# One-core transformer block on Trainium2: projections, transposes and state reads as two row tiles of 64, with new operation orders

## The chip, the cores and the metric

The kernel runs on one core of a Trainium2 chip. A core has TensorE (PE: matmuls and transposes into PSUM, PEld: its weight loads), VectorE (DVE), ScalarE (ACT), GpSimd (POOL), and SyncE (SP), which issues nearly all DMA transfers. The metric is the device time of one execution in microseconds, the median of several runs: 807.32 us before (three runs, 806.09 to 807.65).

## The reference

One transformer block on x of 2048 rows and 512 columns: layer norm with scale and shift from a conditioning vector, attention with a compressive memory, a residual, a second layer norm, a feed-forward part, a residual. The attention has 32 heads of 16 columns and runs in 4 segments of 512 rows:

```python
...
for s in range(N):
    qs, ks, vs = q[:, :, s], k[:, :, s], v[:, :, s]
    logits = jnp.einsum("bhqd,bhkd->bhqk", qs, ks) * scale + mask
    p = _softmax(logits, axis=-1)
    a_dot = jnp.einsum("bhqk,bhkd->bhqd", p, vs)
    pq = phi(qs)
    num = jnp.einsum("bhld,bhde->bhle", pq, M)
    den = jnp.einsum("bhld,bhd->bhl", pq, z)[..., None] + 1e-6
    a_mem = num / den
    o = g * a_mem + (1.0 - g) * a_dot
    pk = phi(ks)
    M = M + jnp.einsum("bhld,bhle->bhde", pk, vs)
    z = z + jnp.einsum("bhld->bhd", pk)
...
h = jnp.einsum("bsf,fd->bsd", relu(x @ w1 + b1) ** 2, w2) + b2
...
```

phi(t) is t + 1 above zero and exp(t) below. The masks are causal within a segment.

## The kernel before

**Tiles and stages.** A unit u (16 of them: segment s = u // 4, column block cc = u % 4) is 8 heads of one segment, that is 128 columns. Products are made from a high and a low part of each operand, so that a product over 128 rows takes three matmuls: high x high, high x low, low x high. For each unit:

- `qk(u)` projects q and k (w = 0, 1): four steps k over 128 rows each, three matmuls of 512 columns per step, into one PSUM bank for q and one for k. ScalarE and VectorE split each bank into the high and low part `sg`; SyncE writes them by 12 transfers (`fill`) into the slots of `ST`, in which two heads of 16 columns lie in each half of 64 partitions. For the memory, ScalarE and GpSimd make phi(q) and phi(k).
- `vproj(s)`, once per segment, projects v for four row blocks t in the same way; ScalarE copies the result into `VT`.
- `a_quad(u, qd)`, for each half of the heads, makes the scores once for the row maxima (`mmA`, 63 rows per matmul, two matmuls beside each other for partitions 0 to 63 and 64 to 127). VectorE reduces; TensorE transposes the maxima, ScalarE negates them (`mt`), and SyncE writes them into `ST` (`rows`).
- `b_quad(u, qd)` makes the scores again with the maxima in a further row (`score`, 64 rows per matmul, in such pairs); ScalarE takes the exponential, GpSimd applies the mask (`select`), `pv` multiplies with v in four column tiles of 32. ScalarE copies the output (`oraw`), TensorE transposes it (`turn_o`), and VectorE divides (`norm`).
- `mem(u)` reads the memory for phi(q) (`read`, 128 rows, 136 columns, four row blocks), transposes phi(k) (`tr`) and updates the memory (`upd`, column tiles of 32).

After that, `wo_tile(g)` multiplies by wo for 16 row blocks, `ln2` makes the second layer norm's operand H2 in one of two buffers, and `ffn1` and `ffn2` run the feed-forward part with w1 and w2 in the same three matmuls per step. 70 warm-up matmuls of a constant stand at the start.

**What sets the order.** The code doesn't run its operations as it writes them. It creates a list of operations (`op`: engine, planned cost, function, priority `pr`, dependencies `after`, buffers to take and give back `get`, `put`). `Plan.run` goes through a written order for each engine (`ORDER`, numbers of operations as they are created), with planned costs, latencies and, for TensorE, a planned cost of each change of mode (`TURN`; F: the whole 128 x 128 array, R: two row tiles of 64, C: four column tiles of 32). `Plan.emit` then calls the functions in that order. On TensorE, VectorE, ScalarE and GpSimd the emitted order is what runs. For SyncE the framework's own scheduler decides. PSUM has eight banks, which the plan hands out; an operation waits on the chip for the banks and buffers that it takes over.

The planned costs are the code's own numbers. The prediction doesn't draw on them.

Of the kernel before, what the change touches and what calls it, by code (L numbers as in the profile page):

```python
# [8 lines left out]
F32 = mybir.dt.float32  # L9
F32R = mybir.dt.float32r  # L10
# [47 lines left out]
8 59 76 43 58 57 16 68 17 53 14 25 35 51 3 33 62 70 10 47 30 34 75 26 20 46 49 69 48 71 19 50 28 11 38 63 74 56 23  # L58
15 67 42 41 65 21 37 39 22 52 73 86 13 105 94 64 88 29 96 60 12 24 72 77 111 40 31-32 36 18 45 117 27 54 123 161 171
162-164 172 165 173 166 174 167 175 168 324 176-178 325-326 330-331 205 213 332 221 206 214-215 327 207 333 216 208  # L60
222-223 229 243 224 480 736 486 240 237 481 197 487 198 488 234 249 482 269 246 199 483 257 352 489 200 254 273
609-610 280 263 271 603 283 260 604 363 288 611 425 266 741 605 276 360 606 612 66 44 372 366 292-294 298 357 301
305 308 55 296 9 369 61 383 313 380 508 751 746 519 427 317-318 386 429 513 319 396 522 436 755-756 439 444 377 757
321 548 758 765 389 516 528 404 550 536 432 533 766-767 406 859 768 525 448 631 639 454 449-450 412 461 642 457 398
920 542 464 469 671 921 414 452 539 645 473 420 474-475 552 636 559 922 477 923 787 861 788-789 545 790 803-804 651
662 567 930-931 555 562 665 805 648 932 992 933 806 422 994 571 656 577 580 673 572 819 659 584 573 596 587 592 833
575 1053-1054 668 1055 675 839 824 597-598 678 682 830 1056 863 1063 600 1064 690 685 827 1065-1066 795-797 836 798
853 850 952 694-696 700 703 707 1339 1125 811-812 1127 813 698 814 957 710 966 715 719 865 847 868 720-721 875 871
844 1186 996 723 1187 856 878 963 972 1188 883 960 986 1189 1196-1197 1334 1198 969 1199 977 887-888 893 980 896 889
998 900 983 1085 1093 908 903 891 1129 989 912 1329 1099 1105 1096 913 1001 1110 914 1131 1004 1090 1008 1116 1016  # L70
1011 1262 916 1102 1344 1113 1020-1022 1026 1119 1218 1033 1258 1348 1358 1029 1036 1223 1349 1260 1024 1122 1359
# [148 lines left out]


class Node:
    __slots__ = ("eng", "dur", "lat", "fn", "pr", "mode", "get", "put", "left", "outs", "seq", "nb", "at")


class Plan:
# [1115 lines left out]
```

## Time and profile before

| quantity | value |
| --- | --- |
| median of three runs | 807.32 us |
| span of the profiled execution | 804.3 us |
| TensorE matmul records, busy | 792.1 us |
| VectorE busy | 537.3 us |
| ScalarE busy | 440.5 us |
| GpSimd busy | 232.9 us |
| matmuls, and as many weight loads | 5289 |
| granted TensorE clock | 1.000 |

The span runs from the first to the last instruction of one profiled execution. The runs are timed without a profile; the profiled execution has no time of its own beside its span. Attention takes the first 460 us or so, with `wo_tile` and the weights' preparation in its last part, and the feed-forward part the rest. A matmul's record lasts longer than its share of TensorE, because matmuls are pipelined; start to start is the measure of what it costs. A float32 matmul (PV, state reads, state update) has two records.

### The profile page before, as it was taken

The page shows a single profiled execution, that of the slowest core. Times are in us where ns is not written, and L with a number is a line of the kernel's source. Part 1 is how long each engine was busy: PE and PEld are TensorE (multiplying, and loading weights), DVE is VectorE, ACT ScalarE, POOL GpSimd, SP SyncE. Part 2 cuts the span into 40 slices and gives each one's busy share as a digit, 9 for nine tenths or more (in the row PEclk, how much of TensorE's full clock was granted, in tenths as well). Part 3 has the DMA queues.
Part 4 walks back from the last instruction along what each step waited for, and adds up shares of the span by engine and source line. Part 5 has one row for each costly group of instructions (what it writes and reads, how often), then busy time and mean ns, then how long its engine had stood idle before and what let it go on. Part 6 is the DMA issues. An engine that isn't in the chain of part 4 may idle for free.

```text
span 804.3 us, 14894 instructions
## 1 busy us (share of the span) xinstructions
PE 792.1 (98%) x5289; PEld 582.3 (72%) x5289; DVE 537.3 (67%) x1425; ACT 440.5 (55%) x908; POOL 232.9 (29%) x314
## 2 busy tenths in 40 slices
PE   8999999999999999999999999999999999999998
PEld 7876666676666756665766678788888888888886
DVE  4688888779877797777999879864433434424223
ACT  1648866789867896677665744543233323322211
POOL 4555535537655684444332211000000000000000
PEclk9999999999999999999999999999999999999999
DMA  9655562324214442434622143230100010001001
GB/s 309 174 135 123 156 206 71 87 74 107 75 47 106 107 103 54 99 74 99 172 66 80 54 145 105 92 92 13 53 1 0 1 53 0 1 1 53 1 1 52
DMA packets 51300, 65.23 MB, mean 81 GB/s; under 512 B 7829, under 2 KB 24985, under 8 KB 51226
## 3 DMA queue, kind: packets, MB, share of 16 engines
q1 hardware_dynamic: 51074, 64.14, 28.6%
q8 instruction: 42, 0.69, 0.3%
q14 instruction: 32, 0.26, 0.1%
q10 hardware_dynamic: 152, 0.13, 0.1%
HBM read 29.91 MB, written 7.34 MB: 46 GB/s over the span
## 4 chain that ended last, share of the span: by engine, by line
PE 80%; DVE 10%; ACT 4%; DMA 3%; issue 2%; SPq 1%; POOL 1%; DVEq 0%; ACTq 0%; POOLq 0%
PE bpv L1015 7%; PE bpf L1291 6%; PE bpf L1290 6%; PE bpf L1292 6%; PE bh L1264 6%; PE bh L1262 6%; PE bh L1263 6%; PE bpb L956 5%; PE ba L799 5%; PE bqk L711 4%; PE bqk L712 3%; PE bqk L713 3%; DVE ba L804 2%; PE bv L770 2%; PE bwop L1101 2%
## 5 line engine op out<-in xcount | busy, mean ns | idle before, releaser
L804 DVE CUSTOM_DVE_ANT_0 ba<-ba,msk 128x512 f32<-128x512 f32 (+2 forms) x384 | 192.5, 532 | 31.0 <-PE ba L799 23.5
L973 ACT ACTIVATE pt<-bpb 128x512 f32<-128x512 f32 x320 | 171.4, 627 | 30.4 <-PE bpb L956 26.6
L1279 DVE TENSOR_TENSOR r<-r 128x512 f32<-128x512 f32 x56 | 38.7, 691 | 122.2 <-ACT rr L1276 122.1
L1272 ACT ACTIVATE r<-bh,b1c 128x512 f32<-128x512 f32 x56 | 38.5, 687 | 138.6 <-PE bh L1264 97.7
L960 POOL TENSOR_SCALAR_AFFINE_SELECT pt<-pt 128x512 f32<-128x512 f32 x128 | 80.1, 645 | 113.1 <-ACT pt L973 86.7
L1291 PE MATMUL bpf<-W,rr 128*128 128x512 f32 x224 | 88.1, 394 | 0.0
L1290 PE MATMUL bpf<-W,rr 128*128 128x512 f32 x224 | 88.1, 393 | 0.0
L1292 PE MATMUL bpf<-W,rr 128*128 128x512 f32 x224 | 87.6, 391 | 0.0
L1015 PE MATMUL bpv<-pt,VT 128*32 128x512 f32 (+3 forms) x1024 | 80.6, 437 | 0.2 <-DVE mx L804 0.2
L956 PE MATMUL bpb<-ST 64*128 64x256 f32 (+2 forms) x512 | 74.5, 353 | 1.3 <-ACT ac L832 0.4
L799 PE MATMUL ba<-ST 63*128 63x256 f32 (+2 forms) x512 | 73.2, 354 | 1.0 <-DVE mx L804 0.7
L956 PEld LDWEIGHTS bpb<-ST 64*128 64x128 f32 x512 | 46.9, 185 | 27.2 <-issue 6.6
L799 PEld LDWEIGHTS ba<-ST 63*128 63x128 f32 x512 | 44.2, 185 | 30.9 <-issue 10.5
L711 PE MATMUL bqk<-HT,WQK 128*128 128x512 f32 (+1 forms) x136 | 58.7, 431 | 0.2 <-DVE sg L732 0.2
L1276 ACT ACTIVATE rr<-r 128x512 fp32r<-128x512 f32 x56 | 35.4, 632 | 41.2 <-PE bpf L1292 40.1
L804 DVE DVE_READ_ACCUMULATOR2_ANT mx<- 128x1 f32 x384 | 54.1, 141 | 0.1
L712 PE MATMUL bqk<-HT,WQK 128*128 128x512 f32 (+1 forms) x136 | 51.9, 382 | 0.7 <-DVE HT L595 0.7
L713 PE MATMUL bqk<-HT,WQK 128*128 128x512 f32 (+1 forms) x136 | 51.8, 381 | 0.0
L1015 PEld LDWEIGHTS bpv<-pt,VT 128*32 128x32 f32 x1024 | 27.2, 109 | 33.7 <-issue 27.3
L1290 PEld LDWEIGHTS bpf<-W,rr 128*128 128x128 f32 x224 | 42.1, 188 | 9.8
L1291 PEld LDWEIGHTS bpf<-W,rr 128*128 128x128 f32 x224 | 42.0, 188 | 9.6
L1292 PEld LDWEIGHTS bpf<-W,rr 128*128 128x128 f32 x224 | 42.1, 188 | 9.4
(160 smaller groups left out, 1614.1 us busy)
## 6 DMA issues: line engine op xcount, KB each, us to landing
ST<-sg SPq DMA_DIRECT2D x192, 128.0 KB
wr<-in_B_w SPq DMA_DIRECT2D x28, 256.0 KB
xt<-in_A_x SPq DMA_DIRECT2D x16, 256.0 KB
wm<-in_w_mod SPq DMA_DIRECT2D x16, 256.0 KB
xw<-in_A_x SPq DMA_DIRECT2D x16, 256.0 KB
o_dram<-on SPq DMA_DIRECT2D x12, 256.0 KB
ot<-o_dram SPq DMA_DIRECT2D x12, 256.0 KB
out<-X SPq DMA_DIRECT2D x12, 256.0 KB
```

Of the source, the lines that this page charges most:

```text
L711: nc.tensor.matmul(p[:, c], wh, HT[:, 0, k, c], start=(k == 0), stop=False)
L712: nc.tensor.matmul(p[:, c], wh, HT[:, 1, k, c], start=False, stop=False)
L713: nc.tensor.matmul(p[:, c], wl, HT[:, 0, k, c], start=False, stop=(k == KD - 1))
L799: nc.tensor.matmul(dst[:, c0:c0 + n], ST[b:b + 63, 0, sl, qt * P:(qt + 1) * P], ST[b:b + 63, 1, sl, :n], start=True, stop=True)
L804: nc.vector.tensor_tensor_reduce(i, i, msk[:, 512 - n:], scale=1.0, scalar=-3e38, op0=ALU.add, op1=ALU.max, accum_out=o)
L956: nc.tensor.matmul(dst, ST[b:b + 64, 1, sl, kb * P:(kb + 1) * P], ST[b:b + 64, 0, sl, q0:512], start=True, stop=True)
L960: nc.gpsimd.affine_select(out=ap, in_=ap, pattern=[[0, ap.shape[1]], [1, P]], compare_op=ALU.is_ge, fill=0.0, base=0, channel_multiplier=-1)
L973: ns = [act(512, lambda j=j: nc.scalar.activation(buf("PPP"[n], pt)[:, i + j], bank(keys[j]), AF.Exp, scale=0.25), pr[slot] + 0.01 + 0.001 ...
L1015: nc.tensor.matmul(bank(o)[32 * hq:32 * hq + 32, q0:q0 + src.shape[1]], v[:, a:a + 32], src, start=start, stop=stop, tile_position=(0, 32 ...
L1290: nc.tensor.matmul(p, rh, FF["W2"][:, f, 0], start=(f == 0), stop=False)
L1291: nc.tensor.matmul(p, rh, FF["W2"][:, f, 1], start=False, stop=False)
L1292: nc.tensor.matmul(p, rl, FF["W2"][:, f, 0], start=False, stop=(f == NF - 1))
```

## The change

What it does:

1. `qk(u)` for u > 0 and `vproj(s)`: each step's three matmuls over 128 rows become six over 64 rows, in pairs for the two halves of the partitions. In the first half of the operation (turn 0), the lower half of the partitions adds into the first bank and the upper half into the second; in turn 1 they swap. The two banks are those of q and k, or of two row blocks of v, which are now made together. Between the turns a one-element copy on ScalarE (`fence`) rewrites an element that turn 1 reads.
2. The transposes of the row maxima, of phi(k) and of the attention output, and the reads of the memory: two row tiles of 64 into two banks. The output of a unit is transposed in one operation for both of its halves instead of two. A half `qd` now has the head pairs qd and qd + 2 in place of 2 qd and 2 qd + 1, and a slot of `ST` follows `slot(u, pp)`.
3. SyncE joins the engines whose order is kept as written.
4. The plan: new costs for some operations and mode changes, dependencies that hold for the plan's start order only (`soft`), a limit for transfers under way, and the rewrite of H2 planned after all of its readers (`F1[s - 2, f]` for every f) instead of the last one.
5. All written orders are new. The warm-up matmuls all stand ahead of the last steps of the first projection.

```diff
...
+    def fence(cell, pr, n):
+        return op("ACT", 0.06, lambda: nc.scalar.copy(cell, cell.bitcast(F32)), pr, after=[n])
+    def slot(u, pp):
+        return (4 * u + 2 * (pp % 2) + pp // 2) % NSLOT
...
+        def half(turn, k):
+            for i, (x, y) in enumerate(((0, 0), (0, 1), (1, 0))):
+                for j in (1, 0) if turn else (0, 1):
+                    w, r = j ^ turn, slice(64 * j, 64 * j + 64)
+                    nc.tensor.matmul(bank(banks[w]), W3(w, k, x, cols.start, cols.stop)[r], HT[r, y, k], start=turn == k == i == 0,
+                                     stop=turn == 1 and k == 0 and i == 2)
...
+            for turn in (0, 1):
+                for k in range(KD):
+                    if turn and not k:
+                        n = fence(HT[64:65, 0, KD - 1, :1], pr[0] + 0.01, n)
+                    n = pe("R", 0.697, lambda turn=turn, k=k: half(turn, KD - 1 - k if turn else k), pr[turn] + 0.002 * k,
...
-        for t in range(4):
-            b = ("v", s, t)
...
+        for t2 in (0, 2):
+            banks = [("v", s, t2 + i) for i in (0, 1)]
+            def mm(turn, k, t2=t2, banks=banks):
+                for i, (x, y) in enumerate(((0, 0), (0, 1), (1, 0))):
+                    for j in (1, 0) if turn else (0, 1):
+                        t, r = j ^ turn, slice(64 * j, 64 * j + 64)
+                        nc.tensor.matmul(bank(banks[t]), HT[r, x, k, (t2 + t) * P:(t2 + t + 1) * P], WVO[r, k, y],
+                                         start=turn == k == i == 0, stop=turn == 1 and k == 0 and i == 2)
...
-        n = pe("F", 0.03, lambda: nc.tensor.transpose(bank(b)[:16, :P], TL[mx], ident), p_tail, after=reds, get=[("#D", b)],
+                nc.tensor.transpose(bank(b[j])[:16, :64], TL[mx][r], ident[r, r])
...
-                    nc.tensor.matmul(qv[:, i], TL[q_][:, t * P:(t + 1) * P], MB[:, cc], start=True, stop=True)
+                        nc.tensor.matmul(bank(banks[j])[:, t * w:(t + 1) * w], TL[q_][r, t * P:(t + 1) * P],
+                                         MB[r, cc, j * w:(j + 1) * w], start=True, stop=True)
...
-                    nc.tensor.transpose(bank(b)[:, t * P:(t + 1) * P], TL[f][:, t * P:(t + 1) * P], ident)
+                        nc.tensor.transpose(bank(b[j])[:, t * 64:t * 64 + 64], TL[f][r, t * P:(t + 1) * P], ident[r, r])
...
-                nc.tensor.transpose(bank(b)[:, t * P:(t + 1) * P], TL[r][:, t * P:(t + 1) * P], ident)
+            for q in (0, 1):
+                for t in range(4):
+                    for j in (0, 1):
+                        w = slice(64 * j, 64 * j + 64)
+                        nc.tensor.transpose(bank(b[j])[:, t * P + 64 * q:t * P + 64 * q + 64], TL["oraw", u, q][w, t * P:(t + 1) * P],
+                                            ident[w, w])
...
-            ln2(s, [z + ST2 * ((s - 1) * NF + 4 + 2 * t) for t in range(4)], [F1[s - 2, NF - 1]] if s > 1 else WOL)
+            ln2(s, [z + ST2 * ((s - 1) * NF + 4 + 2 * t) for t in range(4)], [F1[s - 2, f] for f in range(NF)] if s > 1 else WOL)
...
-    with tc.manual_schedule(engines={mybir.EngineType.PE, mybir.EngineType.DVE, mybir.EngineType.Activation, mybir.EngineType.Pool}):
+    with tc.manual_schedule(engines={mybir.EngineType.PE, mybir.EngineType.DVE, mybir.EngineType.Activation, mybir.EngineType.Pool, mybir.EngineType.SP}):
...
```

More of the change, by code (lines that the diff above doesn't have):

```diff
@@ L63 @@
[L63 to L67, printed above, removed]
@@ L248, in op @@
         n.outs, n.left, n.seq, n.at = [], 0, len(self.nodes), None
-        for a in after:
+        n.soft = {a.seq for a in soft}
+        for a in (*after, *soft):
             if a is not None:
@@ L354, in run @@
                 for o in n.outs:
-                    same = o.eng == n.eng and not n.nb
+                    same = o.eng == n.eng and not n.nb or n.seq in o.soft
                     c = 0 if same else 1 if o.eng != "PE" else 2 if o.mode != "R" else 3
@@ L895, in mem @@
[L895 to L902 removed]
+            banks = [("mr", u, j) for j in (0, 1)]
```

520 lines of the change are left out of this document (273 added, 247 removed), and 10 rows, old and new, of the table ORDER.

## The prediction

> **What bounds the kernel now.** I read the page first: busy shares, slices, chain.
>
> ```profile
> span 804.3 us, 14894 instructions
> PE 792.1 (98%) x5289; PEld 582.3 (72%) x5289; DVE 537.3 (67%) x1425; ACT 440.5 (55%) x908; POOL 232.9 (29%) x314
> ...
> PEclk9999999999999999999999999999999999999999
> ...
> PE 80%; DVE 10%; ACT 4%; DMA 3%; issue 2%; SPq 1%; POOL 1%; DVEq 0%; ACTq 0%; POOLq 0%
> ```
>
> TensorE bounds it: 98% busy, at nine tenths of its clock or more in every slice, and 80% of the chain of waits. But consecutive matmul records overlap (0.40 us long, 0.23 apart), so "busy" also covers time in which the array streams nothing. That time shows only from start to start, which the timeline of TensorE gives (start, length, line, tiles, shape). Four stretches hold what is needed:
>
> ```profile
> 402.65 0.40 PE L1103 MATMUL bwop<-WVO,oT 128*128 128x512 f32 x1
> 402.98 0.50 PE L956 MATMUL bpb<-ST 64*128 64x256 f32 x4
> 403.32 0.63 PE L799 MATMUL ba<-ST 63*128 63x512 f32 x4
> 403.88 2.36 PE L1015 MATMUL bpv<-pt,VT 128*32 128x512 f32 x32
> 406.17 0.73 PE L956 MATMUL bpb<-ST 64*128 64x512 f32 x4
> 406.73 0.46 PE L799 MATMUL ba<-ST 63*128 63x256 f32 x4
> ```
>
> Changes between score pairs and the v projection:
>
> ```profile
> 336.25 0.40 PE L956 MATMUL bpb<-ST 64*128 64x512 f32 x2
> 336.57 0.50 PE L770 MATMUL bv<-WVO,HT 128*128 128x512 f32 x1
> 336.91 0.40 PE L771 MATMUL bv<-WVO,HT 128*128 128x512 f32 x1
> ```
>
> Score pairs in a row:
>
> ```profile
> 76.94 0.51 PE L956 MATMUL bpb<-ST 64*128 64x512 f32 x2
> 77.28 0.40 PE L799 MATMUL ba<-ST 63*128 63x512 f32 x2
> 77.51 0.49 PE L956 MATMUL bpb<-ST 64*128 64x512 f32 x2
> ```
>
> The v projection in a row:
>
> ```profile
> 245.36 0.40 PE L771 MATMUL bv<-WVO,HT 128*128 128x512 f32 x1
> 245.60 0.40 PE L772 MATMUL bv<-WVO,HT 128*128 128x512 f32 x1
> 245.83 0.39 PE L770 MATMUL bv<-WVO,HT 128*128 128x512 f32 x1
> ```
>
> Call 128x128 work F, work in row tiles of 64 (scores) R, work in column tiles of 32 (PV, state update) C. Within F a 512-wide matmul takes 0.235 (245.36, 245.60, 245.83), three of them 0.70. Within R two matmuls of 64 rows and 512 columns together also take 0.235 (77.28 to 77.51). At a change of mode it is more. F to R: 402.65 to 402.98 is 0.33, 0.095 too much, and the first R operation 0.34 where I fit 0.238, 0.10 more: 0.195 in all. R to F: 336.25 to 336.57 is 0.32 and 336.57 to 336.91 is 0.34: 0.19. R to C and back: the three PV steps take 0.86, 0.86 and 0.43, 2.15, but 403.88 to 406.17 is 2.29, 0.14 more; the two score pairs before them take 0.56 instead of 0.47, and the next pairs (406.17 to 406.73) about 0.10 more than their share: 0.33 for both changes. Over all operations I fitted 0.198 (RF), 0.197 (FR), 0.115 (RC), 0.216 (CR) and 0.20 for FC and for CF.
>
> The order list that the kernel prints gives the changes of mode: 69 RF, 63 FR, 42 RC, 48 CR, 15 FC, 9 CF; the trace alternates exactly so. That is 46 us, almost all of it before 480 us. Work within a mode makes 714 us, 487 of it in 696 triples of 0.70. So 760 of the 804 us are work and mode changes; 44 are the start, waits and the tail.
>
> **The change, part by part.** *Mode changes.* Projections, state reads, transposes of phi(k), of the attention output and of the row maxima turn from F to R, and the order is new. I numbered the operations as the code creates them and counted along the new list: 27 RF, 28 FR, 52 RC, 51 CR, 5 FC, 6 CF, 169 instead of 246. The difference: 42 RF and 35 FR fewer, 15.2 us; 10 RC and 3 CR more, 1.8 us; 10 FC and 3 CF fewer, 2.6 us. **-16.0.**
>
> *Projections.* 120 + 64 operations keep their columns: three F matmuls of 512 become three pairs of 64-row matmuls. Rows of score pairs give 0.235 a pair, so 0.70 for 0.70. With twice the instructions and loads I take +0.4; from 0 to +1.3 if all pairs land at 0.237. Untold by these rows: score pairs write with start and stop set, whereas the new pairs add to what stands in PSUM. F matmuls that add keep 0.235, which is the nearest row; the contrary is a rival below.
>
> *Transposes and state reads.*
>
> ```profile
> 244.69 0.60 PE L1043 MATMUL bfin<-ident,oraw 128*128 128x128 f32 x4
> 245.05 0.48 PE L770 MATMUL bv<-WVO,HT 128*128 128x512 f32 x1
> ...
> 264.93 0.62 PE L884 MATMUL bmr<-MB,phi 128*128 128x136 f32 x4
> 265.30 0.48 PE L711 MATMUL bqk<-HT,WQK 128*128 128x512 f32 x1
> ```
>
> An output transpose takes 0.36, two per unit, 32 in all. Afterwards a unit has 16 of half the width, two at a time: between half of 0.71 (if columns count) and all of it (if loads count). I take the middle, 0.53: 16 x 0.18 = -2.9 (-5.7 to 0). The same for phi(k): 12 x (0.36 to 0.27) = -1.0 (-2.1 to 0). State reads are 24 x 0.37; then twelve times eight matmuls of half the width. Half to one and a half of 0.75: I take no difference (-4.5 to +4.5). The transposed row maxima, 32 of 0.03, stay small.
>
> *The turn in the middle.* Every new projection pair swaps its two banks half way, with a one-element ScalarE copy between: 15 for q/k, 8 for v. TensorE's next half waits for it, in order, and so does whatever is listed behind it.
>
> ```profile
> L862 ACT ACTIVATE mt<-bat x32: 248/261/268, 57.6 to 450.5; 16x128 fp32r<-16x128 f32 x32
> ...
> L973 ACT ACTIVATE pt<-bpb 128x512 f32<-128x512 f32 x320 | 171.4, 627 | 30.4 <-PE bpb L956 26.6
> ```
>
> A small ScalarE instruction takes 0.26; the last matmul ends 0.40 after its start, 0.165 beyond its slot; with 0.15 (estimate) for the two hand-overs, 0.6 must be covered. The new list puts 0.29 to 5.5 us of other TensorE work there, under 0.6 in four of the 23, under 0.9 in eleven. ScalarE is in order too: behind half an exponential (0.31) the uncovered sum is 2.5 us, with none 0.5, behind a whole one 6.4. **+2.5.** Uncovered altogether it would be 23 x 0.6 = 14. The copies, 32 further row-maximum copies and 12 further phi(k) copies add some 17 us to ScalarE at 0.26 each; its 45% of idle time hides that.
>
> *SyncE.* Its issues, transfers of segment fills and row maxima among them, now follow the list. At the start this matters:
>
> ```profile
> 3.60 6.63 DMA X1L<-in_A_wq
> 10.25 8.21 DMA wmod<-in_w_mod
> ```
>
> ```profile
> 26.00 0.38 PE L711 MATMUL bqk<-HT,WQK 128*128 128x256 f32 x1
> ```
>
> The first two lines are of the chain of waits: the modulation waits for its weights until 18.46, and wq's transfer stands ahead of them. The third is the timeline's first q/k matmul. The new list issues all modulation weights ahead of wk, wv and wq: the modulation can come earlier by up to wq's 6.63 us, the q/k weights come later. By the list TensorE reaches the first q/k step after 18.0 us of work instead of 20.2, 22 on the clock with the 4 us by which it then lags its list now, not 26. But unit 0's first score also needs its six segment fills on SyncE. I take **-2** (-4 to +3).
>
> *Nothing on the path:* new planner costs, soft dependencies, and the wait for all readers of the feed-forward operand. TensorE runs its list in order, and the last reader comes last on it; what covers the rewrite is the next segment's first product, 56 operations of 0.70. Without that cover, its ScalarE and VectorE steps would show between segments.
>
> **Sum:** -16.0 + 0.4 - 2.9 - 1.0 + 2.5 - 2.0 = -19.0 on the span of 804.3: 785.3. The median shown, 807.32, lies 3.0 above this span: **788.3 us**. What can be told from no change here is 0.2%, 1.6 us. Adding the bounds in root-sum (3 for the output transposes, 4.5 reads, 4 turns, 4 start, and 11 for the waits of a new order, a quarter of the 44): about 13 either way, 775 to 801.
>
> **Rivals.** *B, the gain is partly given back as waits.*
>
> ```profile
> 180.00:200.00 20.00, 19.96 (x225) 12.20 (x224) 18.95 (x64) 18.81 (x43) 15.42 (x22) 1.00 0.44 108
> ...
> 380.00:400.00 20.00, 19.85 (x160) 13.61 (x161) 19.38 (x57) 13.54 (x28) 7.92 (x10) 1.00 0.65 180
> 400.00:420.00 20.00, 20.00 (x167) 13.11 (x164) 18.46 (x55) 12.95 (x26) 6.70 (x10) 1.00 0.26 80
> 420.00:440.00 20.00, 20.00 (x147) 13.05 (x146) 19.07 (x62) 12.96 (x27) 4.44 (x8) 1.00 0.24 81
> ```
>
> Columns: stretch, its length, then busy time of TensorE, its loads, VectorE, ScalarE, GpSimd. In these 80 us VectorE has 18.5 to 19.4 of 20 in use. If it can't give more, a share of 80/460 of the gain, 3.3 us, is lost there, and waits beside them double it: 795. Against it: the stretches on either side can take VectorE's work, which is 67% over the span. *C, the waits shrink as well.* The planner now charges GpSimd and VectorE steps what they take, so the new order could lose a third of the 30 us or so of waits (44 less the start and the tail): 778. No row shows it.
>
> *D, slower: pairs that add to PSUM don't fully overlap.* Place: the 184 projection operations. Full overlap 0.70, none 1.40. It decides from 19/184 = 0.10 us each, a loss of 15% of the overlapped rate; at half overlap, +0.35 x 184 = +64: 852. For it: no row has adding row tiles. Against it: score pairs overlap fully, and column tiles of PV add at full rate (0.86 for four of 512). The Trainium skill (TensorE: Matmul & The Clock Gate, Measured speedup vs the span model) reports 3.07x for four row tiles instead of 4x. By that factor an operation would take 0.91 and the kernel some 827 us; the trace's score pairs, 0.235 for two where F has 0.235 for one, disagree.
>
> *E, slower: the turns stall.* If ScalarE's queue holds the copy behind instructions that wait themselves, each turn costs more; the gain is gone at 0.83 us more for each of the 23. At 1.5 more: 823. Against it: 11 turns have over a microsecond of cover. *That the change doesn't do what it says* is no case for the modes, which can be counted; for SyncE's order it is: little moves, and the 2 us are missing, within the forecast's range.
>
> **How the numbers follow.** Forecast 0.60, B 0.14, C 0.12, D 0.05, E 0.09. Faster: forecast, C, and nearly all of B: 0.84. Slower: D, E and a little of B: 0.13. Same 0.03. For the range I leave out D, E's upper part and C's lower end: 775 to 805.
>
> **What would show it.** Right: about 169 changes of mode on TensorE, projection pairs 0.235 apart start to start, a first q/k matmul near 22 us, attention's last PV step some 19 us earlier than now, a feed-forward part as long as now. Wrong: projection pairs over 0.27 apart (D); idle TensorE ahead of the second halves with ScalarE as releaser (E); VectorE or ScalarE over 95% with TensorE waiting for them in the middle (B).

## The result, and the profile after

| | before | after |
| --- | --- | --- |
| median of 20 runs each | 807.57 us (806.09 to 811.02) | 803.85 us (800.68 to 807.82) |
| span of the profiled execution | 804.3 us | 805.9 us |

The ratio of the times is 0.9951, 95% interval 0.9939 to 0.9964: 0.5% faster, 3.7 us, where 19 us were forecast. 803.85 lies inside the range of 775 to 805, at its end. The profiled execution of the changed kernel is one of its longest (807.64) and that of the kernel before one of its shortest (the times lie 1.7 us above the spans, so 804.3 answers to 806.0), so the spans differ by +1.6 us where the medians differ by -3.7, and some 5 us of what is longer after in the parts below belong to these two executions.

The page of the changed kernel, the lines that answer to those of before:

```profile
span 805.9 us, 16640 instructions
PE 777.3 (96%) x6145; PEld 591.0 (73%) x6145; DVE 532.0 (66%) x1425; ACT 447.8 (56%) x975; POOL 230.5 (29%) x314
...
PEclk9999999999999899998999999999999999999998
...
PE 76%; DVE 6%; ACT 5%; DMA 5%; issue 3%; SPq 3%; POOL 1%; DVEq 0%; ACTq 0%; POOLq 0%
```

Three things are new: TensorE is busy for 15 us less, its granted clock falls under nine tenths in three slices, and the chain that ended last has more of DMA and of SyncE's queue (SPq) in it.

The windows view (length, then busy time of TensorE, its loads, VectorE, ScalarE, GpSimd; clock; DMA) of the changed kernel at the joints of the segments, where one segment's attention runs out and the next one's projections begin:

```profile
160.00:180.00 20.00, 17.59 (x199) 11.90 (x191) 15.35 (x46) 16.14 (x37) 12.58 (x17) 1.00 0.39 93
...
260.00:280.00 20.00, 18.11 (x168) 11.67 (x164) 11.49 (x41) 17.34 (x39) 11.21 (x14) 0.84 0.34 80
360.00:380.00 20.00, 16.74 (x162) 10.36 (x163) 17.91 (x53) 14.43 (x31) 9.59 (x12) 0.90 0.55 157
380.00:400.00 20.00, 20.00 (x166) 12.43 (x159) 17.76 (x50) 12.36 (x26) 6.61 (x8) 0.92 0.52 132
```

and of the kernel before:

```profile
160.00:180.00 20.00, 19.85 (x191) 14.17 (x184) 15.75 (x56) 16.58 (x37) 7.37 (x15) 1.00 0.30 78
...
260.00:280.00 20.00, 20.00 (x178) 14.13 (x176) 16.09 (x55) 16.45 (x36) 13.79 (x19) 1.00 0.44 108
360.00:380.00 20.00, 19.85 (x136) 12.39 (x135) 15.36 (x45) 14.71 (x34) 8.11 (x11) 1.00 0.43 104
```

In these three stretches TensorE had no matmul running for at most 0.15 of 20 us before; now it is 1.9 to 3.3. From 60 to 80 it is busy for 17.16 of 20 us where it was for 19.55.

I fitted the start-to-start times of all of TensorE's operations again, in the way of the prediction: a duration for each kind, a price for each kind of change of mode, and the rest as waits. "Tail" runs from the start of the last operation (three matmuls) to the end of the span.

| us | before | after | difference | forecast |
| --- | --- | --- | --- | --- |
| work within a mode | 713.5 | 709.0 | -4.5 | -3.5 |
| changes of mode (246, 169) | 46.1 | 33.5 | -12.6 | -16.0 |
| waits | 38.3 | 49.7 | +11.4 | +2.5 and -2.0 |
| tail | 4.8 | 12.2 | +7.4 | 0 |
| sum | | | +1.7 | -19.0 |

At the prices of the kernel before, the 169 changes are 30.1 us and the waits 53: the fit gives R to C 0.182 where it was 0.115, and can't tell a dearer change from a wait that stands beside it; 3 us or so can stand on either line. The first two lines bring 17.1 of the 19.5 us that were forecast for them; the last two take it back. With the medians' -3.7 us in place of +1.7, and the other three lines as they are, the waits grow by about 6 us instead of 11.4 (an estimate).

**The tail.** SyncE's stores at the end of the changed kernel, from the timeline (start, length, engine, line, operation, count; the second column is that of the whole group):

```profile
725.12 2.41 SPq L1363 DMA_DIRECT2D out<-X  x5
796.84 0.81 SPq L1363 DMA_DIRECT2D out<-X1L  x2
797.69 0.45 SPq L1363 DMA_DIRECT2D out<-X  x1
798.24 0.40 SPq L1363 DMA_DIRECT2D out<-X1L  x1
798.68 1.64 SPq L1363 DMA_DIRECT2D out<-X  x3
800.36 0.64 SPq L1363 DMA_DIRECT2D out<-X1L  x1
801.05 1.33 SPq L1363 DMA_DIRECT2D out<-X  x2
```

X1L is the last segment, X the others. After five stores at 725 none is issued for 69 us, and ten are left when the last tile is ready. The kernel before has four left there, all of X1L, and the first of them is issued 0.9 us ahead of the last matmul's start (799.94), here 2.7 us behind it (794.17):

```profile
799.04 2.37 SPq L1302 DMA_DIRECT2D out<-X1L  x4
```

VectorE's list has a part in it. The last additions of the changed kernel, then the matmul that ends last:

```profile
794.60 2.55 DVE L1361 TENSOR_TENSOR X1L<-bpf,X1L 128x256 f32<-128x256 f32 x5 [5.35 <-PE bpf L1353]
```

```profile
794.17 0.39 PE L1353 MATMUL bpf<-W,rr 128*128 128x512 f32 x1
```

The group begins with a half tile, 256 columns: tile 3 of the segment, the one that TensorE finishes last. VectorE waits 5.35 us for it while tiles 1, 0 and 2 lie finished.

**The clock.** Windows of 3.41 us of the changed kernel, laid on the edges of the clock's record (the column after the engines is the granted clock); each stretch at half clock has the window ahead of it:

```profile
72.41:75.83 3.42, 1.41 (x12) 0.62 (x12) 2.51 (x8) 1.65 (x5) 3.42 (x4) 1.00 0.08 26
75.83:79.24 3.41, 3.41 (x50) 1.74 (x53) 0.00 (x0) 2.23 (x5) 1.40 (x2) 0.50 0.00 0
270.38:273.80 3.42, 2.57 (x22) 1.16 (x18) 3.28 (x15) 2.54 (x6) 2.52 (x2) 1.00 0.21 43
273.80:280.63 6.83, 5.79 (x37) 2.96 (x36) 5.09 (x19) 6.43 (x14) 3.17 (x5) 0.50 0.04 13
372.78:376.20 3.42, 0.90 (x9) 0.76 (x9) 3.38 (x8) 2.54 (x6) 1.79 (x2) 1.00 0.23 75
376.20:383.03 6.83, 6.76 (x44) 4.12 (x48) 5.31 (x15) 4.67 (x12) 3.22 (x4) 0.50 0.29 79
```

TensorE is busy for 1.41, 2.57 and 0.90 of 3.42 us, then it gets half its clock for one or two such windows: 17 us, in which what it does takes twice as long. At most 8.5 us of the waits in the table are this. The kernel before has none ahead of its end.

**The longest waits** of the changed kernel's TensorE:

```profile
PE bpb L1008 <- DVE sg L768: 2.5, 1, 2.5
PE bpb L1008 <- DMA ST<-mt: 2.0, 1, 2.0
```

The columns are the whole wait, the number of times and the longest. The first stands at 372, the second at 73, both ahead of a stretch at half clock.

### The profile page after: what moved, and what is told of

Read it like the earlier page. It is cut to its first block, busy times and chain, and to the rows that moved or that the text cites. A ratio compares the mean times of both kernels' runs of the same rounds, so it can differ in the third digit from the quotient of the medians.

```text
span 805.9 us, 16640 instructions
## 1 busy us (share of the span) xinstructions
PE 777.3 (96%) x6145; PEld 591.0 (73%) x6145; DVE 532.0 (66%) x1425; ACT 447.8 (56%) x975; POOL 230.5 (29%) x314
## 4 chain that ended last, share of the span: by engine, by line
PE 76%; DVE 6%; ACT 5%; DMA 5%; issue 3%; SPq 3%; POOL 1%; DVEq 0%; ACTq 0%; POOLq 0%
PE bqk L732 8%; PE bpv L1067 7%; PE bpf L1352 6%; PE bpf L1351 6%; PE bpf L1353 6%; PE bh L1323 6%; PE bh L1325 6%; PE bh L1324 6%; PE bpb L1008 5%; PE ba L839 5%; PE bv L805 4%; SPq L784 2%; ACT pt L1025 2%; PE bwop L1162 2%; DMA wr<-in_B_w 1%
## 5 line engine op out<-in xcount | busy, mean ns | idle before, releaser
L844 DVE CUSTOM_DVE_ANT_0 ba<-ba,msk 128x384 f32<-128x384 f32 (+2 forms) x384 | 192.6, 532 | 36.6 <-PE ba L839 29.1
L732 PE MATMUL bqk<-HT,WQK 64*128 64x512 f32 x720 | 102.3, 396 | 0.1
L1008 PE MATMUL bpb<-ST 64*128 64x256 f32 (+2 forms) x512 | 79.7, 354 | 5.2 <-DVE sg L768 2.5
L1067 PE MATMUL bpv<-pt,VT 128*32 128x512 f32 (+3 forms) x1024 | 84.3, 450 | 0.4 <-ACT pt L1025 0.3
L839 PE MATMUL ba<-ST 63*128 63x256 f32 (+2 forms) x512 | 75.6, 345 | 2.5 <-ACT pt L1025 1.0
L732 PEld LDWEIGHTS bqk<-HT,WQK 64*128 64x128 f32 x720 | 68.9, 185 | 10.9 <-issue 1.0
L1008 PEld LDWEIGHTS bpb<-ST 64*128 64x128 f32 x512 | 50.8, 189 | 25.7 <-issue 4.7
L839 PEld LDWEIGHTS ba<-ST 63*128 63x128 f32 x512 | 49.6, 187 | 22.8 <-ACT pt L1025 6.7
L805 PE MATMUL bv<-WVO,HT 64*128 64x512 f32 x384 | 54.0, 396 | 0.0
```

The source lines that it names most:

```text
L732: nc.tensor.matmul(bank(banks[w]), W3(w, k, x, cols.start, cols.stop)[r], HT[r, y, k], start=turn == k == i == 0, stop=turn == 1 and k == ...
L805: nc.tensor.matmul(bank(banks[t]), HT[r, x, k, (t2 + t) * P:(t2 + t + 1) * P], WVO[r, k, y], start=turn == k == i == 0, stop=turn == 1 and ...
L839: nc.tensor.matmul(dst[:, c0:c0 + n], ST[b:b + 63, 0, sl, qt * P:(qt + 1) * P], ST[b:b + 63, 1, sl, :n], start=True, stop=True)
L844: nc.vector.tensor_tensor_reduce(i, i, msk[:, 512 - n:], scale=1.0, scalar=-3e38, op0=ALU.add, op1=ALU.max, accum_out=o)
L1008: nc.tensor.matmul(dst, ST[b:b + 64, 1, sl, kb * P:(kb + 1) * P], ST[b:b + 64, 0, sl, q0:512], start=True, stop=True)
L1067: nc.tensor.matmul(bank(o)[32 * hq:32 * hq + 32, q0:q0 + src.shape[1]], v[:, a:a + 32], src, start=start, stop=stop, tile_position=(0, 32 ...
```

## The experiments

The theory after reading the two traces: the gain in work and modes is there in full; two lists that end in a wrong order took 7 us of it at the end; the rest went into waits at the joints and into the half clock that follows them. A rival for the tail was that the last transfers set it in any order, a rival for the waits that SyncE's kept order costs all along, and a rival for the modes that a change costs less than fitted. The brackets behind each time hold its ratio to the kernel before in the same session and the 95% interval; an interval is 0.2% to either side, so that gains of 1.5 us and less can't be told.

### The tail: tail_sorted, tail_both

```diff
-"SP": ... out 1 3, 2 1, 0 1, 0 0, 0 3, 1 2, 3 1, 3 2, 2 2, 3 3, 1 1, 2 0, 0 2, 3 0, 1 0, 2 3
+"SP": ... out 0 0, 0 2, 0 1, 0 3, 1 1, 1 3, 1 0, 1 2, 2 2, 2 3, 2 0, 2 1, 3 3, 3 0, 3 2, 3 1
```

(numbers of the list given as names: out segment tile)

> The changed kernel with one thing altered: SyncE's last sixteen issues, the output stores, stand in the order in which VectorE finishes their tiles (segments 0, 1, 2, 3). Theory (SyncE's kept list gives the gain back at the end): in the changed kernel TensorE's last operation starts at 793.7 and the span ends 12.2 us later, 4.8 in the kernel before, because ten stores stand behind 'out 3 1' and 'out 3 2' and are issued one after another from 796.84 on. Sorted, four stores are left for the end and the tail is about 5 us: 6.5 to 7.5 us less, a median near 797. Rival (the tail is made by the transfers of the last tiles themselves, or by the clock, and the order is hidden): within 1.5 us of the 803.85 measured. The rest of the trace, TensorE's last start at 793 to 794 included, stays as it is by both.

799.83 us (0.9907, 0.9889 to 0.9924), 4 us less than the changed kernel: more than the rival allows, less than the theory. The tail is 8.5 us (789.5 to 798.0). VectorE and SyncE in it:

```profile
790.43 2.55 DVE L1361 TENSOR_TENSOR X1L<-bpf,X1L 128x256 f32<-128x256 f32 x5 [5.35 <-PE bpf L1353]
```

```profile
793.00 1.79 SPq L1363 DMA_DIRECT2D out<-X1L  x4
```

VectorE's wait is unchanged, and that is the missing part.

```diff
-"DVE": ... out 3 3, 3 0, 3 2, 3 1, 3 3
+"DVE": ... out 3 1, 3 0, 3 2, 3 3, 3 3
-"SP": ... out 3 3, 3 0, 3 2, 3 1
+"SP": ... out 3 1, 3 0, 3 2, 3 3
```

The last four stores follow VectorE's new order. The stores of the earlier segments change places among themselves as well; they are long done by then.

> As tail_sorted, and VectorE's last additions (segment 3's tiles) in the order in which TensorE finishes them, 3 1, 3 0, 3 2, 3 3, instead of 3 3 first; the stores on SyncE the same. In tail_sorted TensorE's last operation starts at 789.5, VectorE waits 5.35 us for the last tile and adds all four from 790.43, SyncE's first store of X1L issues at 793.00, and the span ends at 798.0: a tail of 8.5 us where the kernel before has 4.8 and its first addition at 798.32, 1.6 us ahead of TensorE's last matmul. Theory (VectorE's list holds the other half of the lost tail): first addition 1 us or more ahead of TensorE's last matmul, tail 4.5 to 5.3, 3 to 4 us less than tail_sorted: 796 to 797. Rival (the stores' landing sets the end in any order): tail 8 or more, 799 to 800.

795.11 us (0.9840, 0.9819 to 0.9861). The tail is 4.8 us (789.8 to 794.6), that of the kernel before. The first addition starts ahead of TensorE's end now, and the first store with it:

```profile
787.24 0.69 DVE L1360 TENSOR_TENSOR X1L<-bpf,X1L 128x512 f32<-128x512 f32 x1 [1.95 <-PE bpf L1352]
789.28 2.12 DVE L1360 TENSOR_TENSOR X1L<-bpf,X1L 128x512 f32<-128x512 f32 x4 [1.35 <-PE bpf L1352]
```

The tail is settled: both edits together bring 8.7 us between the medians, the 7.4 of the fit and about 1 more. This version beats both kernels.

### SyncE's kept order by itself: before_sp_kept, sp_free

```diff
-with tc.manual_schedule(engines={PE, DVE, Activation, Pool}):
+with tc.manual_schedule(engines={PE, DVE, Activation, Pool, SP}):
```

in the kernel before, and the reverse in the changed kernel.

> One part alone: the kernel before, with SyncE's issues kept in its plan's order too and nothing else changed. Its list ends with the stores of segments 0, 1, 2, 3 in that order, so no store of an early segment stands behind the last ones. Theory (keeping the order is harmless where the list is right; what costs is the new list's tail and its tight row-maximum issues): a tail of 4.5 to 5.5 us and a median within 3 us of 807.6, either side. Rival (an order kept by hand costs on SyncE in itself, since every issue that waits holds those behind it): 4 us or more above 807.6, with TensorE waiting for segment fills or row maxima all through attention.

808.93 us (1.0015, 0.9998 to 1.0032): no difference that can be told. Keeping an order costs nothing that shows, and brings nothing where the rest stays.

> One part of the change undone: SyncE's order is no longer kept, everything else is as in the changed kernel (lists, row tiles, waits). Theory (the kept order costs at the end, through the stores, and is worth little elsewhere): SyncE issues the stores as they become ready, a tail of 8 to 9 us (VectorE's list still has the last tile first), 2 to 5 us less than 803.85. Rival 1 (the kept order is worth what the change wanted from it, an earlier start and steadier fills, 4 us or more): above 804 in spite of the shorter tail. Rival 2 (the tail is VectorE's alone): within 1.5 us of 803.85, tail above 11.

802.68 us (0.9932, 0.9910 to 0.9954): 1.2 us less than the changed kernel, too little for the theory, and the two intervals overlap. The trace shows two effects that go against each other. The tail falls from 12.2 to 6.9, and TensorE's waits at the start and for the row maxima grow:

```profile
PE bpb L1008 <- DMA ST<-mt: 5.0, 3, 2.7
PE bqk L726 <- POOL WQK L682: 3.3, 1, 3.3
```

against 2.0 and 0.9 in the changed kernel. The first score pair stands at 45.07, in the changed kernel at 40.97. With the new lists, then, the kept order is worth some 4 us ahead of the tail (5.3 us of tail less 1.2 in all, an estimate from the medians), and gives about as much back at the end.

### The price of the modes: proj_full_rows

```diff
-for j in (1, 0) if turn else (0, 1):
-    w, r = j ^ turn, slice(64 * j, 64 * j + 64)
-    nc.tensor.matmul(bank(banks[w]), W3(...)[r], HT[r, y, k], ...)
+nc.tensor.matmul(bank(banks[turn]), W3(...), HT[:, y, k], ...)
```

and the same for v.

> The changed kernel with the row tiles of the projections undone and everything else kept: each of the 184 projection steps is three matmuls of 128 rows into one bank (first half of an operation into one bank, second half into the other) instead of three pairs of 64 rows; list, banks and fences stay. Along the same list the changes of mode go from 169 to 426 (128 more RF, 129 more FR). Theory (a change of mode costs TensorE about 0.2 us wherever it stands): 128 x 0.198 + 129 x 0.197 = 51 us more, less what falls into the 50 us of waits: 840 to 858. Rival (a change costs little and the fitted prices were waits that stand beside it): under 20 us more, below 824. A second reading, of the claim that pairs of row tiles that add to the same banks do not overlap: if they did not, this kernel would gain on its projections, 184 steps above 0.75 us each in the changed kernel; at 0.694 a step here and there, they overlap.

841.27 us (1.0414, 1.0395 to 1.0432): 37.4 more than the changed kernel, at the lower end of the theory. The fit gives 78.7 us for 426 changes, where the changed kernel has 33.5 for 169: 45.2 for 257, 0.18 each. The waits fall from 49.7 to 38.2. So a change costs about what was fitted, and a part of it comes out of the waits: 11.5 of 45.2 by the two traces, 7.8 by the medians (45.2 less 37.4). Read backwards, a sixth to a quarter of what a removed change saves would come back as waits. The projection steps take 0.69 to 0.70 us in both forms.

### The joints: joints, tail_qk, act_joints, wo_pool, act_wo, fill_pool, fill_pool_all

The first pair of moves goes for the two longest waits:

```diff
 "SP":  ... 8 of the 12 fills of unit 2,
+mt 0 1,
 the other 4
-mt 0 1
 "DVE": ...
+qklo 15 1,
 wo 3, red3 13 0 1, wo 2, wo 3
-qklo 15 1
```

> The changed kernel with two instructions moved in the lists: on SyncE the row maxima of unit 0's second quad go ahead of the last four fills of unit 2 (they were ready at 68.7 and issued at 71.4 to 72.8), and on VectorE the low part of unit 15's k goes ahead of the output weight's casts that wait for their load. Theory (two joints make two long waits of TensorE, 2.2 us at 72.7 and 2.7 us at 371.9, and each is followed by a stretch at half the clock, 75.83 to 79.24 and 376.20 to 383.03, that costs up to half its length again): both waits fall under 0.7 us, both stretches are gone, the one at 273.80 stays; 5 to 9 us less, 795 to 799. Rival (the waits move: what follows waits for ScalarE or VectorE anyway): less than 2.5 us, 801.3 or more. If the waits go and the stretches at half clock stay, the clock does not follow these waits.

807.2 us (0.9990, 0.9972 to 1.0007): 3 us more than the changed kernel. The theory fell. In place of the wait for the row maxima stands a longer one:

```profile
73.99 0.49 PE L1007 MATMUL bpb<-ST 64*128 64x512 f32 x1
77.14 1.06 PE L1007 MATMUL bpb<-ST 64*128 64x512 f32 x5 [2.65 <-ACT pk L959]
```

and ScalarE shows where it comes from:

```profile
76.22 0.59 ACT L765 CAST sg<-bqk 128x512 fp32r<-128x512 f32 x1 [3.50 <-DMA ST<-sg]
76.71 0.38 ACT L959 COPY pk<-bpkt 128x256 f32<-128x256 f32 x1
```

The cast of unit 3's q needs the one staging buffer `sg`, which the last four fills of unit 2 still read; everything else on ScalarE stands behind it for 3.5 us. The twelve fills take 0.61 to 0.67 us of SyncE each. Whichever of the two is issued second, the maxima or the last fills, is waited for.

From here on the moves are made on tail_both, which takes the tail out of the comparison. First the move on VectorE alone:

> tail_both with the one move on VectorE of the kernel 'joints': the low part of unit 15's k ahead of the output weight's casts. In 'joints' the two moves together were 3 us slower: the move on SyncE turned a wait of 2.2 us for the row maxima into one of 3.3 us (ScalarE held 3.5 us by unit 2's last fills), while near 372 the wait of 2.72 became 1.45 + 1.39 and the slices from 360 to 400 had 7.3 us of waits instead of 9.1. Theory A (the stretch 360 to 400 is bound by VectorE and ScalarE together, so a move in one list gains part of it): 1 to 2.5 us less than tail_both, 794 to 795.5. Theory B (waits only move there): within 1 us of tail_both. A loss of over 1 us speaks for neither.

796.26 us (0.9859, 0.9842 to 0.9876): nothing. Then two moves on ScalarE ('oraw 7 1' and an exponential ahead of 'qkhi 11', a copy of 'pk 5' ahead of 'relu 7 1'), the subtractions for wo on GpSimd instead of VectorE (`nc.vector.tensor_tensor` to `nc.gpsimd.tensor_tensor` in `load_wo`), and both:

> tail_both with three ScalarE instructions moved in its list: 'oraw 7 1' and the exponential that follows it go ahead of the two casts 'qkhi 11', which in tail_both wait 1.03 us at 270 until the last fill of unit 10 has read the staging buffer; and the second copy of 'pk 5' goes ahead of 'relu 7 1', which idles ScalarE 0.5 us at 174. Theory (at the joints TensorE waits for what stands on ScalarE behind an instruction that itself waits): the waits of TensorE at 270.5 (1.34) and 174.4 (1.25) fall under 0.5 each, the half-clock stretch at 272.8 goes or moves, 1.5 to 4 us less than tail_both's 795.1: 791 to 793.6. Rival (ScalarE, at 8 to 10 of 10 us busy there, is the bound, so another wait takes its place): within 1 us of 795.1.

> tail_both with the four subtractions that make the output weight's low halves on GpSimd instead of VectorE (same values). In tail_both VectorE is busy 17.0 of 20 us from 360 to 380, eight operations of 0.69 us for the weight among them, and TensorE's waits there add up to 9.3 us. Theory (at this joint VectorE is the bound, since its work for the output weight falls into a stretch that it has no room in): 2.5 us of VectorE's time are freed, the wait at 367.9 (2.91) falls by 1 to 2.5 us and what follows with it, 1.5 to 4 us less than tail_both: 791 to 793.6. Rival (what sets the end there is the output weight's load, issued on SyncE behind nine fills, or ScalarE): within 1 us of 795.1; GpSimd, with 1.23 us for each, would be the one waited for.

> act_joints and wo_pool together. If both theories hold and the joints are far enough apart not to share a wait: the sum of the two gains, 788 to 792. If either is a wait that only moves, the gain of the other alone; if TensorE's lead over ScalarE and VectorE is what the joints use up, less than the sum.

795.52, 795.33 and 794.49 us: ratios 0.9847 (0.9826 to 0.9869), 0.9846 (0.9832 to 0.9859) and 0.9842 (0.9827 to 0.9857), all of them tail_both's 0.9840. The waits named are gone or much shorter, at one place with another of 1.0 us in its stead, and the sums stay: 47.3 us in tail_both, 47.1, 48.8 and 45.2 here, each known to some 2 us (the spans, with the same work, changes and tail, are 794.6, then 796.1, 796.9 and 792.1). At the last joint, 360 to 385, the view of waits shows it changing hands. tail_both:

```profile
PE bpb L1007 <- DVE sg L767: 2.6, 1, 2.6
PE bmr L931 <- DVE mx L843: 0.7, 1, 0.7
```

tail_qk, then wo_pool:

```profile
PE bpb L1007 <- ACT pt L1024: 1.0, 2, 0.6
PE ba L838 <- DVE mx L843: 1.0, 1, 1.0
```

```profile
PE ba L838 <- DVE oT L1196: 1.4, 1, 1.4
...
PE bpb L1007 <- DVE sg L767: 0.6, 1, 0.6
```

Last, a third of the fills of units 2, 6, 10 and 14 were given to GpSimd's queue, without and with the moves on VectorE and ScalarE:

> tail_both with four of the twelve fills of units 2, 6, 10 and 14 issued by GpSimd's queue instead of SyncE's, at the same places of the plan's time. Theory (SyncE's issue rate, through the one staging buffer, sets when ScalarE's next casts can start at the joints): the buffer comes free up to 2.6 us earlier there, ScalarE's wait for the fills at 270 (1.03 us) and TensorE's longest wait at 368 (2.91) shrink by half or more, waits of 360 to 380 under 6 us (9.3), 1.5 to 5 us less than tail_both: 790 to 793.6. Rival (the lists' order, whatever the fills do): within 1 us of 795.1. If GpSimd's issues hold its own selects back, TensorE waits for these and the time is above 796.

> fill_pool with the moves of tail_qk (VectorE) and of act_joints (ScalarE). Theory (issue rate and list order are two links of one chain, so that mending one alone moves the wait to the other): the moves, worth nothing by themselves (796.3 and 795.5), now bring 1 us or more beyond fill_pool; below 792. Rival: the same as fill_pool within 1 us.

795.9 and 795.47 us (0.9846, 0.9819 to 0.9874, and 0.9852, 0.9831 to 0.9874). At the last joint, 360 to 385, the two longest waits, 2.6 and 0.7 in tail_both, are now 1.1 and 1.0, and the time is the same:

```profile
PE bmr L931 <- DVE mx L843: 1.1, 1, 1.1
PE bpb L1007 <- DVE sg L766: 1.0, 1, 1.0
```

Both theories fell.

### Whose time is short: dve_light, act_light, both_light

```diff
-nc.vector.tensor_tensor_reduce(i, i, msk[:, 512 - n:], ...)
+m = n // 2 if n > P else n
+nc.vector.tensor_tensor_reduce(i[:, :m], i[:, :m], msk[:, 512 - n:512 - n + m], ...)
```

> tail_both with part of VectorE's work left out: the row maxima run over the first half of their columns (256 of 512, 192 of 384), some 55 us less of VectorE's time, all of it in attention; lists, waits and every other engine's work stay. Theory A (VectorE's capacity makes the waits at the joint of 360 to 380, and part of the others): waits there fall from 9.3 to under 4 us and those of 160 to 200 and 260 to 300 by a third of their 8.5 and 7.2; 6 to 10 us less than tail_both's 795.1, 785 to 789. Theory B (ScalarE and the order of single instructions make them): within 2 us of 795.1. What VectorE frees in stretches in which TensorE does not wait brings nothing by either.

791.62 us (0.9798, 0.9769 to 0.9827), 3.5 less than tail_both, whose interval overlaps a little: between the theories. VectorE is busy for 477.1 us (532.5 in tail_both), and the waits at 360 to 380 are still 7.0 us; in all they are 43.5 instead of 47.3. But at that joint VectorE was not relieved, as the windows of tail_both and then dve_light show:

```profile
360.00:380.00 20.00, 16.34 (x149) 9.37 (x147) 16.97 (x40) 14.78 (x30) 10.09 (x11) 0.83 0.47 128
```

```profile
360.00:380.00 20.00, 16.95 (x156) 9.47 (x153) 17.44 (x46) 16.60 (x36) 10.87 (x12) 0.91 0.48 139
```

VectorE is busy for 17.44 of 20 us there, 16.97 in tail_both. So the run speaks against VectorE's capacity as the main cause over all of attention, and leaves it open at this joint. (Maxima over half of the scores no longer bound all exponents, so this isn't offered as a version.)

> tail_both with part of ScalarE's work left out: each exponential of the scores runs over the first 256 of its 512 columns, and GpSimd writes ones into the rest; some 80 us less of ScalarE's time, some 100 more of GpSimd's; lists stay. Theory B (ScalarE's capacity and what stands behind one another on it make the waits at 160 to 200 and 260 to 300): these fall from 8.5 and 7.2 to under 4 each, 360 to 380 keeps at least 5 of its 9.3; 6 to 10 us less than 795.1. Theory A (VectorE makes them): within 2 us of 795.1. Theory C (neither alone, both engines run out at the same joints): 2 to 5 us less here and in dve_light. If GpSimd's added work is waited for, the time is above 797 and tells nothing.

798.22 us (0.9893, 0.9873 to 0.9914). ScalarE is down to 387.2 us, and TensorE's waits are 47.1, about those of tail_both; 3.7 us of them are for GpSimd's selects now. By its own expectation this tells little: GpSimd's added writes are waited for. What can be said is that ScalarE's 60 us less left the 7.6 us at 360 to 380 standing, where ScalarE is busy for 10.78 of 20 us instead of 14.78.

> dve_light and act_light together: what of the waits is left when neither engine is short. Theory (capacity at the joints): waits from 40 to 480 fall to 10 us or less from 31, no stretch at half clock before the end, 12 to 20 us less than tail_both, 775 to 783. Rival (the lists' order and SyncE's issues of 0.61 to 0.67 us each make most of them): 5 us or less below the better of the two, and the waits near 27, 41, 61 and 457 to 493 as before by both.

794.45 us (0.9843, 0.9816 to 0.9869), waits 47.6, of which 7.0 for GpSimd's selects. The experiment missed its question in the same way.

### The half clock: clock_fill

At the head of 's1 12 1 0', and likewise of 'at 13 0' (r: the rows of half j):

```diff
+for _ in range(6):
+    for j in (0, 1):
+        nc.tensor.matmul(p[j][:, :P], ident[r], ident[r], start=True, stop=True)
```

> tail_both with twelve idle-time matmuls of 64 rows and 128 columns (the identity times itself, overwritten at once) at the head of each of two operations that stand beside TensorE's longest waits, 's1 12 1 0' and 'at 13 0'; the result is the same. In tail_sorted TensorE waits 2.81 us just after the first and 1.58 us at the second, and the granted clock is 0.5 from 371.81 to 378.63. Theory (the clock is halved because TensorE idles most of a stretch of some 3.4 us there, and the half clock costs up to 3.4 us by itself): TensorE busy through both waits, the clock 1.0 from 340 to 400, the stretches near 177 and 273 as before; 1.5 to 3.4 us less than tail_both. Rival (the clock falls for another reason, or the time at half clock lies in waits anyway): the half-clock stretch is still there, or the time is within 1 us of tail_both or above it, since the fillers push what stands behind them back.

796.65 us (0.9855, 0.9835 to 0.9876; runs from 793.34 to 798.49), tail_both 795.11 (793.15 to 797.57): by the medians, nothing. The traces show the place itself. tail_both, then clock_fill, windows over the same stretch of the clock:

```profile
371.78:378.61 6.83, 6.19 (x40) 3.92 (x44) 5.72 (x18) 4.68 (x12) 3.29 (x5) 0.50 0.34 83
```

```profile
371.78:378.61 6.83, 6.83 (x80) 4.32 (x77) 5.61 (x12) 5.97 (x15) 3.16 (x5) 1.00 0.35 89
```

The stretch at half clock is gone, and from the same PV step to the same score pair (366.06 to 379.87, and 365.03 to 376.73) it takes 11.7 us instead of 13.8. So the half clock here hangs on TensorE's idleness. The 2.1 us are not its price alone: the matmuls put in take time of their own, and a wait of 0.7 us for VectorE's `mx` is gone as well. That no gain shows in the medians stays unexplained; the runs of one kernel lie 4 to 5 us apart, and the profile sees one of them.

## Why the prediction was wrong

Of the 19.0 us forecast, 3.7 came. Of the missing 15.3, 7.4 are the tail, which the prediction left at nothing, about 5.5 the waits, and 3.4 the changes of mode, less 1.0 us that the work brought beyond its forecast (by the table, with the waits at +6). Attention's last PV step starts at 457.18, 6.8 us earlier than before (464.02) where some 19 were expected; the feed-forward part is as long as it was, as expected.

**Modes: right.** 246 to 169 changes, as counted from the list; proj_full_rows puts a price of 0.18 on each where 0.197 was taken. **Work within a mode: right, by other parts.** -4.5 for -3.5. An output transpose unit of 16 half-width transposes took 0.465, not 0.53 (-4.0 in all, forecast -2.9); phi(k)'s 0.20 to 0.21, not 0.27 (-1.9, forecast -1.0); a state read 0.81, not 0.75 (+0.7, forecast 0). The groups of the q/k and v projections and a stretch of the timeline with two steps in a row:

```profile
L732 PE MATMUL bqk<-HT,WQK 64*128 64x512 f32 x720 | 102.3, 396 | 0.1
L805 PE MATMUL bv<-WVO,HT 64*128 64x512 f32 x384 | 54.0, 396 | 0.0
```

```profile
147.63 1.56 PE L732 MATMUL bqk<-HT,WQK 64*128 64x512 f32 x12
149.02 0.40 PE L1008 MATMUL bpb<-ST 64*128 64x512 f32 x2
```

Twelve matmuls from 147.63 to 149.02: 1.39 us, 0.695 for a step. **Rival D is refuted:** pairs that add to the same banks overlap in full, two for the time of one. The Trainium skill's 3.07x for four row tiles (TensorE: Matmul & The Clock Gate, Measured speedup vs the span model) doesn't carry over to two tiles of 64; here it is 2x of 2.

**The turn in the middle: too dear.** +2.5 was taken for 23 turns. The last number of a group's row is TensorE's idle time ahead of all its matmuls, second halves among them: 0.1 and 0.0 us. In the trace the second half of an operation starts 0.67 us or more after the last matmul of the first, so that all 23 turns were covered. **Rival E is refuted.** The 0.15 us taken for the two hand-overs had no row; in the traces TensorE to ScalarE takes 0.04 us and ScalarE to TensorE 0.05 to 0.15. ScalarE's 67 further instructions cost it 7.3 us (440.5 to 447.8), not 17.

**SyncE: the step that failed.** The prediction read the head of SyncE's new list and gave it -2 (-4 to +3), and the end of the kernel nothing. The head was read rightly. The first q/k matmul stands at 23.22 (26.00 before, 22 forecast; 26.00 less 20.2 is a lag of 5.8 us and not 4, and 18.0 with that lag is 23.8):

```profile
23.22 0.36 PE L724 MATMUL bqk<-HT,WQK 128*128 128x256 f32 x1
```

The first score pair comes 5.5 us earlier, though the weights' split on GpSimd holds a step of the projection for 0.95 us. Before, then after:

```profile
46.48 0.80 PE L799 MATMUL ba<-ST 63*128 63x256 f32 x8
```

```profile
40.97 0.69 PE L839 MATMUL ba<-ST 63*128 63x256 f32 x8
```

By sp_free, some 4 us of that are the kept order's. What failed is the other end. The prediction didn't read the tail of the same list, which was printed, nor that of VectorE's. Reading 'out 1 3' at the head of the stores and 'out 3 1' before nine others would have shown that six stores of finished segments stand behind the last segment's, and 'out 3 3' ahead of 'out 3 1' that VectorE starts with the tile that comes last. Worked out from the rows: six stores more at 0.4 to 0.65 us are 3 us; and SyncE's first store of the ten is of tile 1, which VectorE, held by tile 3, adds last but one, some 2 us after it starts: 5 of the 7.4 us. tail_sorted took 3.7 us off the tail by the stores' order, tail_both another 3.7 by VectorE's. The plan couldn't see either: the end that it works out (`self.end`) is that of TensorE's operations alone.

**Waits of the new order: a bound of 11 either way, with nothing taken.** They came out at +11.4 in the profiled execution and +9.0 in that of tail_both, at the edge of the bound, and about +6 by the medians. **Rival C is refuted:** the waits grew. **Rival B had the direction right, and the place wrong** (its 795 is where the kernel without the tail stands, which is luck): it put the loss into 180 to 200 and 380 to 440, where VectorE is busy throughout, and there TensorE hardly waits; it waits at 160 to 180, 260 to 280 and 360 to 380, where VectorE is busy for 15.35, 11.49 and 17.91 of 20 us. VectorE's capacity makes a smaller part of the waits at most, by dve_light, which left out 55 us of VectorE's work and saved 3.5; at 360 to 380 it stays open.

**What stays open.** Why the sum of the waits holds at 44 to 49 us, whichever link is mended. proj_full_rows would fit a chain through SyncE's fills, the one staging buffer, ScalarE's and VectorE's lists and the banks, which TensorE runs into at each joint when it gets ahead, but no run shows this chain as a whole; each of five edits mended one link, and the view of waits named the next. A second staging buffer, which would cut the chain at its middle, wasn't tried. What ScalarE's time has to do with it ahead of 360 is not settled, since GpSimd's added work covered the answer.

## What to carry to other kernels

When a list that was searched by a model is now kept on one more engine, read its last entries before its first: what the model doesn't price, here all that comes after TensorE's end, is in no order at all, and one early wait holds every finished store behind it. Price removed work on the busiest engine at less than its duration where that engine runs in step with the others; here a sixth to a quarter of it came back as waits. And a wait that a trace names is the last link of a chain: before a gain is booked for mending it, look at what was late next.

## What the runs showed of the hardware

In the 18 profiled executions 41 stretches at half clock begin in attention after the first 40 us, none of them in the kernel before; each is 3.41 or 6.83 us long, and all of one execution lie on one grid of 3.41 us. By the records' busy time on that grid, every window at full clock in which TensorE was busy for under 56% (18 of them) was followed by half clock; 22 more stretches followed windows with 59 to 77%, one a window with 87%. 46 windows of 57 to 77% have none behind them. So the share of a window seems to matter, not the length of one gap: the 2.0 us at 73 were enough. The Trainium skill (TensorE: Matmul & The Clock Gate, HAM oscillation) gives the rule as no idle gaps over about 3.4 us; the window's length agrees with the trace, the rule is too mild for it. Over the changed kernel's 20 runs the mean clock goes from 0.985, with the three times of 805.34, 807.64 and 807.82, to 0.991, with 801.25 and 801.84 (the shortest, 800.68, has 0.989): a part of a kernel's spread goes with the number of such stretches. Which of the two comes first, a longer wait or a longer stretch, these means don't show.
